# The rounded parts of q and k made on GpSimd instead of ScalarE in 22 attention steps

## The chip, the core and the metric

The kernel runs on one core of a Trainium2 chip. A core has five engines, each with its own instruction queue, that meet only at semaphores: TensorE (PE in the profile, with its weight loads as PEld), VectorE (DVE), ScalarE (ACT), GpSimd (POOL) and SyncE (SP), which here only issues DMAs. The metric is the time of one execution on the device, in microseconds. The kernel before took 996.66 us, the median of three runs (995.94 to 996.84).

## The reference

Attention with a sigmoid in the place of the softmax, and behind it a feed-forward layer with a squared ReLU:

```python
# q, k, v: (8, 12, 448, 64)
scores = scale * np.matmul(q, k.transpose(0, 1, 3, 2)) - np.log(S)
attn = 1.0 / (1.0 + np.exp(-scores))
attn_out = np.matmul(attn, v)
# x: 3584 tokens of 768; w_in (768, 2048), w_out (2048, 768)
h = x @ w_in
r = np.maximum(h, 0.0)
g = s * (r * r) + b
return g @ w_out
```

All of it is in float32 precision. The change touches only the attention.

## The kernel before

TensorE multiplies matrices in a rounded 32-bit format here (`F32R`, fp32r in the profile). To keep float32's precision, an operand x is split in two parts: hi, which is x rounded to that format, and lo = x - hi. A product is then made of three matmuls, hi by hi, hi by lo and lo by hi (`PARTS`, line 39).

The work has three stages. First comes attention, in 24 steps; during it the weights of the feed-forward layer, which come in 64-bit floats, are converted, combined and stored as parts, by ACT and DVE, in jobs that a hand-written plan gives to the steps (`at_step`, `ticks`, lines 534 to 540). Then the feed-forward layer is computed for one block of 512 tokens (lines 825 to 875), while the conversion ends. Last, it is computed for twice three blocks of 512 tokens (lines 992 to 1303), in a scheme that needs fewer products at the price of sums. The last two stages use neither q nor k.

A step of attention handles one batch and four of its heads. Its q and k lie in one tile of 128 x 2 x 2 x 448 numbers (`load`, line 387): two heads in the two halves of the partitions, two pairs of heads, q and k. The tile is fetched by one DMA on SP's queue two steps ahead (line 669) into a pool of two buffers. From it, one step ahead, the two parts are made:

- `parts_hi` (lines 409 to 413) allocates the tiles hi and lo, 128 x 1664 each (q, and the first three chunks of 128 keys; the rest of the keys is multiplied unsplit), and writes hi. The pool `hl` has one buffer for each (line 379), so hi of the next step can be written only when the scores of this step are done.
- `parts_lo` (lines 415 to 417) writes lo on DVE (the subtraction is `sub`, line 198).

The first two steps have their parts made on DVE (`parts_dve`, line 419). The other 22 (`TWO`, line 61) use the two functions above.

In step n (lines 650 to 687) instructions are issued in this order, and each engine takes its own in that order:

1. DVE's planned jobs of the step (line 652).
2. `scores` (line 439): TensorE makes 36 score matmuls from hi and lo in pairs (line 459), and ACT the sigmoids of the six chunks (lines 434 and 436).
3. `parts_hi` for step n + 1 (line 666), on ACT behind the six sigmoids.
4. ACT's planned jobs (line 667): converting weights (line 223), rounding weights and sums (lines 273 and 331).
5. DMAs on SP: q and k of step n + 2 (line 669), weights, and stores of finished weights.
6. TensorE's attention times v (line 495), the last scores of step n + 1 (line 481, whose sigmoid ACT does next), and the rest of attention times v (line 504).
7. `parts_lo` for step n + 1 (line 683), on DVE.
8. `store_x` (line 509): DVE takes two results from PSUM (line 512), SP stores them.

So on DVE lo stands behind the planned jobs and ahead of the two copies of line 512. GpSimd has no instruction in this loop. Synchronisation is derived from the tiles: whoever reads hi waits for whoever wrote it.

Of the kernel before, what the change touches and what calls it, by code (L numbers as in the profile page):

```python
# [102 lines left out]
def sigmoid_attention_relu2_ffn(  # L103
# [10 lines left out]
    nc = tc.nc  # L114
# [291 lines left out]
    def flat(x):  # L406
        return x.rearrange("p i x s -> p i (x s)")[:, :, :NX]

    def parts_hi(b, t, ld_):

        hi, lo = (hl.tile([P, 2, NX], F32R, tag=h, name=f"qk{h}_{b}_{t}") for h in "hl")
        nc.scalar.copy(hi, flat(ld_[0]))  # L412
        ld_.append((hi, lo))

    def parts_lo(ld_):
# [234 lines left out]
    for n, (b, t) in enumerate(quads):  # L650
# [4 lines left out]
        if n == 0:  # L655
            parts_dve(*quads[1], loaded[1], [(i, slice(NX)) for i in range(2)])
            ticks(0, "DVE")
            firsts = []

            def between():  # L660
                firsts.append(scores_last(*quads[0], loaded[0]))
                ticks(0, "ACT")

        else:
            if n + 1 in TWO:
                parts_hi(*quads[n + 1], loaded[n + 1])
            ticks(n, "ACT")
# [674 lines left out]
```

## Time and profile before

| what | value |
|---|---|
| median of three runs | 996.66 us (995.94 to 996.84) |
| span of the profiled execution | 995.0 us |
| attention: first 24 steps | to about 245 us |
| length of a step | 9.99 us |
| granted TensorE clock | 1.000 |
| copies of line 412 | 22, 35.6 us in all, 1617 ns in the mean |
| subtractions for lo in those steps | 22, 1892 ns in the median |
| DMA of a tile of q and k | 896 KB, 7.2 us to landing in the median |

The profile is of one execution. Its own time is known by its span, from the first to the last instruction; the median of the timed runs is 1.66 us above it. PE, PEld, DVE, ACT, POOL and SP are the engines. "L412" is line 412 of the kernel. A row of groups reads: line, engine, operation, output<-inputs, shapes, number of instructions | busy us in all, mean ns of one | idle us of the engine just before them, and who ended most of that idle time. A row of the timeline reads: start, duration, engine, line, operation, output<-inputs, shapes, count, and in brackets the idle time before it and its releaser. A row of waits reads: who waited <- for whom: us in total, times, longest. A row of the chain of waits reads: start, duration, engine, tile and line. A row of windows reads: the stretch and its length, then each engine's busy us (and number of instructions), the granted clock, the DMA engines' busy share and GB/s.

In the tile names qk is the raw tile of q and k, qkh is hi, qkl is lo, psc are scores, a are attention weights, pav is attention times v and xo its copy in SBUF; st and wf are weights in conversion, and t and w are sums and parts of weights.

### The profile page before, as it was taken

The page shows a single profiled execution, that of the slowest core. Times are in us where ns is not written, and L with a number is a line of the kernel's source. Part 1 is how long each engine was busy: PE and PEld are TensorE (multiplying, and loading weights), DVE is VectorE, ACT ScalarE, POOL GpSimd, SP SyncE. Part 2 cuts the span into 40 slices and gives each one's busy share as a digit, 9 for nine tenths or more (in the row PEclk, how much of TensorE's full clock was granted, in tenths as well). Part 3 has the DMA queues.
Part 4 walks back from the last instruction along what each step waited for, and adds up shares of the span by engine and source line. Part 5 has one row for each costly group of instructions (what it writes and reads, how often), then busy time and mean ns, then how long its engine had stood idle before and what let it go on. Part 6 is the DMA issues. An engine that isn't in the chain of part 4 may idle for free.

```text
span 995.0 us, 13973 instructions
## 1 busy us (share of the span) xinstructions
PE 991.2 (100%) x5288; PEld 783.6 (79%) x5288; DVE 840.6 (84%) x933; ACT 616.1 (62%) x687; POOL 0.2 (0%) x4
## 2 busy tenths in 40 slices
PE   9999999999999999999999999999999999999998
PEld 4555555555888888888888888888888888888887
DVE  5999999999889976799999898996465789889787
ACT  7999999998877575575455444443455336543432
POOL 0000000000000000000000000000000000000000
PEclk9999999999999999999999999999999999999999
DMA  8788898999899999999686678978666676677773
GB/s 327 282 332 324 311 372 316 418 359 402 306 404 360 371 391 407 381 334 368 215 276 204 210 260 309 305 249 267 202 207 198 205 208 197 209 239 226 229 240 123
DMA packets 101826, 287.18 MB, mean 289 GB/s; under 512 B 10240, under 2 KB 20608, under 8 KB 101760
## 3 DMA queue, kind: packets, MB, share of 16 engines
q1 hardware_dynamic: 101472, 285.84, 81.9%
q8 instruction: 42, 0.69, 0.3%
q10 hardware_dynamic: 288, 0.46, 0.1%
q14 instruction: 24, 0.20, 0.0%
HBM read 198.18 MB, written 88.08 MB: 288 GB/s over the span
## 4 chain that ended last, share of the span: by engine, by line
PE 100%; DVE 0%; issue 0%
PE o L1269 31%; PE h L1137 31%; PE pav L495 11%; PE psc L459 9%; PE po L811 6%; PE ph L606 6%; PE psc_l L481 2%; PE pav L504 2%; PE psc L465 0%; PE idle L527 0%; DVE C_t L198 0%
## 5 line engine op out<-in xcount | busy, mean ns | idle before, releaser
L1137 PE MATMUL h<-s_1h,wu 128*128 128x512 f32 x480 | 143.0, 379 | 0.0
L1137 PE MATMUL h<-s_0h,wu 128*128 128x512 f32 x480 | 143.0, 379 | 0.0
L436 ACT ACTIVATE a<-psc,nls 128x896 f32<-128x896 f32 x120 | 113.4, 1020 | 11.0 <-PE psc L459 8.3
L495 PE MATMUL pav<-a,v 128*64 128x448 f32 x576 | 113.8, 543 | 0.0
L1137 PEld LDWEIGHTS h<-s_0h,wu 128*128 128x128 f32 x480 | 90.7, 189 | 12.8
L1137 PEld LDWEIGHTS h<-s_1h,wu 128*128 128x128 f32 x480 | 90.7, 189 | 12.8
L1009 ACT COPY G<-h 128x1024 f32<-128x1024 f32 x48 | 48.9, 1019 | 82.3 <-PE h L1137 56.6
L901 ACT ACTIVATE G<-G,b_sb,s_sb 128x1024 f32<-128x1024 f32 x48 | 59.7, 1244 | 57.6 <-DVE G L898 57.0
L1137 PE MATMUL h<-s_0l,wu 128*128 128x512 f32 x240 | 91.0, 379 | 0.0
L1137 PE MATMUL h<-s_1l,wu 128*128 128x512 f32 x240 | 91.0, 379 | 0.0
L495 PEld LDWEIGHTS pav<-a,v 128*64 128x64 f32 x576 | 39.1, 137 | 62.6 <-issue 55.7
L195 DVE TENSOR_TENSOR G<-G,h 128x1024 f32<-128x1024 f32 x40 | 48.8, 1219 | 35.9 <-PE h L1137 34.7
L1269 PE MATMUL o<-g_3h,wu 128*128 128x512 f32 (+1 forms) x244 | 76.4, 376 | 0.0
L1269 PE MATMUL o<-g_0h,wu 128*128 128x512 f32 x240 | 76.3, 379 | 0.0
L1269 PE MATMUL o<-g_1h,wu 128*128 128x512 f32 x240 | 76.3, 379 | 0.0
L1269 PE MATMUL o<-g_2h,wu 128*128 128x512 f32 x240 | 76.3, 379 | 0.0
L811 PE MATMUL po<-g,w 128*128 128x512 f32 x288 | 64.8, 379 | 0.0
L811 PEld LDWEIGHTS po<-g,w 128*128 128x128 f32 x288 | 54.4, 189 | 8.0 <-DVE g L198 0.4
L606 PE MATMUL ph<-x0h,w 128*128 128x512 f32 x192 | 59.6, 380 | 0.0
L459 PE MATMUL psc<-qkh 64*128 64x448 f32 x282 | 53.8, 378 | 0.0
L198 DVE TENSOR_TENSOR qkl<-qk,qkh 128x1664 fp32r<-128x1664 f32 (+3 forms) x26 | 44.9, 1726 | 9.8 <-ACT qkh L412 9.5
L1269 PEld LDWEIGHTS o<-g_3h,wu 128*128 128x128 f32 x244 | 45.9, 189 | 6.4
(154 smaller groups left out, 2053.7 us busy)
## 6 DMA issues: line engine op xcount, KB each, us to landing
wu<-wd SPq DMA_DIRECT2D x240, 512.0 KB, 4.3
wd<-t SPq DMA_DIRECT2D x36, 768.0 KB, 8.0
qk<-qk_t SPq DMA_DIRECT2D x23, 896.0 KB, 7.2
st<-w_out SPq DMA_DIRECT2D x16, 768.0 KB, 8.6
st<-w_in SPq DMA_DIRECT2D x16, 768.0 KB, 8.6
wd<-w SPq DMA_DIRECT2D x16, 768.0 KB, 5.6
v<-v_t SPq DMA_DIRECT2D x24, 448.0 KB, 5.8
xd<-xo SPq DMA_DIRECT2D x24, 448.0 KB, 5.2
```

The costliest lines, as they stand in the source:

```text
L195: nc.vector.tensor_tensor(o, x, y, op=ALU.add)
L198: nc.vector.tensor_tensor(o, x, y, op=ALU.subtract)
L436: nc.scalar.activation(a, psc[:, :, :S], AF.Sigmoid, bias=nls, scale=SCALE)
L459: nc.tensor.matmul(o[j][:, :S], two[wi][r, i, cols], paired(two[xi][r, i, :S]), start=m == 0, stop=m == 2,)
L481: nc.tensor.matmul(psc[half[i], j, :S].rearrange("p (b a) -> p a b", a=2), x[r, i, 1, 3 * P :], x[r, i, 0, :], start=True, stop=True,)
L495: nc.tensor.matmul(pav[i][r, :S], ld_[1][:, 3 * i + c, j, :], a[i, c][:, j, :], start=c == 0, stop=False,)
L606: nc.tensor.matmul(ph, w[:, k, wi, kc * P : (kc + 1) * P], paired(x0[h][xi][:, cc, :]), start=m == 0, stop=m == 3 * NCC - 1,)
L811: nc.tensor.matmul(pos[e], w[:, k, wi, kc * P : (kc + 1) * P], paired(g[:, gi, :]), start=first and i == 0, stop=last and i == 2,)
L901: nc.scalar.activation(x, x, AF.Identity, bias=b_sb, scale=s_sb)
L1009: nc.scalar.copy(g(m, h), bk)
L1137: nc.tensor.matmul(bk[:, j], wt[:, j, wi, c * P : (c + 1) * P], paired(opd[i][xi][:, c, :]), start=i == ch[0] and m == 0, stop=m == 3 * KC ...
L1269: nc.tensor.matmul(o, wt[:, f, wi, e * P : (e + 1) * P], paired(g[gi][:, f, tk]), start=(end or i == ch[0] and p == 0) and f == 0 and m == ...
```

## The change

One line differs. The rounded copy hi of the next step's q and k is issued on GpSimd; what it reads, what it writes and where it stands in the program are the same.

```diff
     def parts_hi(b, t, ld_):
 
         hi, lo = (hl.tile([P, 2, NX], F32R, tag=h, name=f"qk{h}_{b}_{t}") for h in "hl")
-        nc.scalar.copy(hi, flat(ld_[0]))
+        nc.gpsimd.tensor_copy(hi, flat(ld_[0]))
         ld_.append((hi, lo))
```

`parts_hi` is called from one place, line 666, in steps 1 to 22, for the steps after them. So ACT's queue goes from the sixth sigmoid straight to its planned jobs, GpSimd gets 22 instructions, and `parts_lo` on DVE waits for GpSimd where it waited for ACT.

## Prediction

> **What bounds the kernel now.** I read the page first: span, busy time, and the slices.
>
> ```profile
> span 995.0 us, 13973 instructions
> PE 991.2 (100%) x5288; PEld 783.6 (79%) x5288; DVE 840.6 (84%) x933; ACT 616.1 (62%) x687; POOL 0.2 (0%) x4
> ...
> DVE  5999999999889976799999898996465789889787
> ACT  7999999998877575575455444443455336543432
> POOL 0000000000000000000000000000000000000000
> ```
>
> TensorE is busy throughout. ACT's 62% is a mean over unlike stages: in the first ten slices, the attention, ACT and DVE are both near full. POOL runs four instructions in all. So I read the stage, in windows of one attention step each; the first and last of 21, and their sum:
>
> ```profile
> core 0: us, PE busy (x) PEld busy (x) DVE busy (x) ACT busy (x) POOL busy (x), PEclk, DMA share, GB/s
> 26.40:36.39 9.99, 9.99 (x80) 5.38 (x76) 9.71 (x13) 9.35 (x12) 0.00 (x0) 1.00 0.80 298
> ...
> 226.16:236.15 9.99, 9.99 (x80) 5.39 (x76) 8.77 (x11) 9.45 (x12) 0.00 (x0) 1.00 1.03 405
> sum 209.75, PE 209.75 PEld 113.21 DVE 196.29 ACT 200.78 POOL 0.00; mean PE 9.99 PEld 5.39 DVE 9.35 ACT 9.56 POOL 0.00
> ```
>
> A step lasts 9.99 us, TensorE fills it at full clock, ACT has 0.43 us over (9.99 - 9.56) and DVE 0.64 (9.99 - 9.35). Three engines are within 7% of each other, so an engine that is given work, or is held up, can become the bound at once. The timeline of one step shows what hangs on what:
>
> ```profile
> 126.33 0.46 PE L459 MATMUL psc<-qkh 64*128 64x448 f32 x2
> 126.44 1.16 DVE L512 COPY xo<-pav 128x448 f32<-128x448 f32 x2
> 127.51 0.95 DVE L225 SCALAR_TENSOR_TENSOR wf<-st,wf 128x768 int32<-128x768 int32 x1
> 128.49 0.59 DVE L228 TENSOR_SCALAR st<-st 128x768 int32<-128x768 int32 x1
> 128.52 0.51 SPq L396 DMA_DIRECT2D qk<-qk_t  x1
> 129.11 0.96 DVE L232 SCALAR_TENSOR_TENSOR st<-st 128x768 f32<-128x768 uint32 x1
> 129.76 0.35 PE L459 MATMUL psc<-qkh,qkl 64*128 64x448 f32 x2
> 130.11 0.96 DVE L235 SCALAR_TENSOR_TENSOR wf<-st,wf 128x768 f32<-128x768 f32 x1
> 130.99 0.95 DVE L198 TENSOR_TENSOR t<-t 128x768 fp32r<-128x768 f32 x1
> 132.82 1.61 ACT L412 CAST qkh<-qk 128x1664 fp32r<-128x1664 f32 x1
> 133.44 0.55 DVE L219 TENSOR_SCALAR wf<-st 128x768 int32<-128x768 int32 x1
> 134.47 1.89 DVE L198 TENSOR_TENSOR qkl<-qk,qkh 128x1664 fp32r<-128x1664 f32 x1 [0.47 <-ACT qkh L412]
> 136.37 0.46 PE L459 MATMUL psc<-qkh 64*128 64x448 f32 x2
> 136.66 0.35 PE L459 MATMUL psc<-qkl,qkh 64*128 64x448 f32 x2
> ```
>
> ACT's copy ends at 132.82 + 1.61 = 134.43, DVE's subtraction for the second part (qkl) starts 0.04 later, ends at 136.36, and TensorE begins the next step's scores at 136.37; its second pair needs qkl. The chain copy, subtraction, scores is all but on the path, though TensorE itself still sets the pace.
>
> How late may qkl be? The steps whose subtraction started late tell: 9.98 to 9.99 us after the last is the rule, and one came 10.18 us after it (114.44 to 124.62, about 0.19 late). The attention-times-v matmuls after it came 10.03 us after those before, where 9.99 is the rule:
>
> ```profile
> 114.44 1.89 DVE L198 TENSOR_TENSOR qkl<-qk,qkh 128x1664 fp32r<-128x1664 f32 x1 [0.49 <-ACT qkh L412]
> 124.62 1.89 DVE L198 TENSOR_TENSOR qkl<-qk,qkh 128x1664 fp32r<-128x1664 f32 x1 [0.33 <-ACT qkh L412]
> ```
> ```profile
> 110.09 4.66 PE pav L495 x24
> 120.08 4.66 PE pav L495 x24
> 130.11 4.66 PE pav L495 x24
> 140.10 4.66 PE pav L495 x24
> ```
>
> So 0.19 us late cost TensorE 0.04: the slack is about 0.15 us a step.
>
> **The change part by part.** What goes from ACT, and what DVE idles for it:
>
> ```profile
> L412 ACT CAST qkh<-qk 128x1664 fp32r<-128x1664 f32 x22 | 35.6, 1617 | 0.0
> L198 DVE TENSOR_TENSOR qkl<-qk,qkh 128x1664 fp32r<-128x1664 f32 (+3 forms) x26 | 44.9, 1726 | 9.8 <-ACT qkh L412 9.5
> L624 DVE CAST x0h<-x0l 128x1536 fp32r<-128x1536 f32 x1 | 1.0, 951 | 0.0
> ```
>
> ```profile
> ACT a L436 <- PE psc L459: 8.3, 21, 0.6
> ```
>
> Removed: 22 copies of 1.617 us, 35.6 us of ACT. Worth nothing by itself: ACT waits for TensorE's scores at the start of a step already (8.3 us in 21 steps, by the waits), and TensorE has no gap in the windows above that an earlier sigmoid could fill. At most the 0.04 us of the one late step returns.
>
> Added: 22 copies on GpSimd, whose queue holds nothing else in the stage, so its waits block nothing behind them. When can one start? Its input was requested a step ahead (128.52 for use in the step from 136.37) and takes 7.2 us in the median, so it is there at 135.7. Its output buffer is single, and is free when the last score pair has read it: 129.76 + 0.35 = 130.11 in the step shown.
>
> ```profile
> qk<-qk_t SPq DMA_DIRECT2D x23, 896.0 KB, 7.2
> ```
>
> DVE is through with the work ahead of the subtraction at 133.44 + 0.55 = 133.99. So the copy may take 3.9 us at no cost, and up to 134.47 + 0.15 - 130.11 = 4.5 us before TensorE waits, if it runs beside DVE without touching it.
>
> What one copy lasts on GpSimd, no row shows: its four instructions are memsets of one element. From the nearest rows: below, DVE's one-input cast scaled, 0.951 x 1664 / 1536 = 1.03 us; above, twice ACT's row, 3.23 us, a factor I choose because these rows for such elementwise work already lie nearly a factor of two apart. I take 1.89 us, the slowest instruction of this shape in the trace (the subtraction), since the copy reads and writes the same array at one number at a time as that one does. All these fit in 4.5 us.
>
> [...]
>
> So duration alone costs nothing. What decides is whether the copy takes time from DVE. Between 130.11 and 133.99 DVE works without a break, and every instruction there reads its operands from the same memory as the copy. The rows say how much DVE takes in: the 768-element subtraction at 130.99 reads two operands in 0.95 us, and the one-input cast of 1536 elements also takes 0.95. In both, some 1536 numbers in 0.95 us: DVE draws on two streams in either form, so it has no spare one to give up for free. If the two engines take turns, it does not matter who goes first: DVE either stands while the copy runs, or the copy waits until DVE has nothing to do but wait for it (133.99) and then runs alone. Either way a copy's length is added to DVE's step.
>
> [...]
>
> The sum: DVE must find 22 x 1.89 = 41.6 us. It has free what it idles for qkh today, 9.5 us (the other 0.2 us of a step are gaps between dependent instructions, which stay). The slack of qkl, 22 x 0.15 = 3.3 us, goes against two hand-overs a step (0.04 us was the one from ACT above; two engines taking turns can hardly have cheaper ones, so 2 to 4 us); I set both to nothing. Added: 41.6 - 9.5 = 32.1 us. The profiled execution spans 995.0; the median of the timed runs, 996.66, lies 1.66 above it, which I keep: 995.0 + 1.66 + 32.1 = 1028.7 us. A step becomes about 9.99 + 32.1 / 22 = 11.45 us. Behind the late subtraction on DVE stand the two evictions (L512) and the weight conversion; who waits are TensorE's next scores. The stages after attention are not touched.
>
> With the ends of the copy's price: 1.03 gives 22.7 - 9.5 = 13.2, so 1009.9; 3.23 gives 71.1 - 9.5 = 61.6, so 1058.2.
>
> **The rivals.** First, not slower: the copy runs beside DVE undisturbed. It then lasts from 130.11 to about 132.0, the subtraction starts at about 134.0 instead of 134.47, and nothing follows, for TensorE is still busy with attention times v until 136.3: 996.6 us. For it: no row shows the two engines in conflict, and 1.89 is far under 4.5. Against: it must be nearly complete. A loss to DVE of 0.67 us a step (22 x 0.67 = 14.7, less 9.5 free and 3.3 slack, leaves 2) already shows, a third of one copy. From that point it decides.
>
> Second: undisturbed, but the copy lasts over 4.5 us. At 5.5 it would be 22 x 1.0 more, 1018.7 us; it needs a price 2.9 times the chosen one. The step would be set by GpSimd, with DVE idle.
>
> Third: faster. Lightening ACT by 35.6 us would have to bring TensorE forward, which has nothing to regain in the windows; I see under 1 us. That the copy does not go to GpSimd I leave out: the line names the engine.
>
> **How the numbers follow.** Turns between DVE and GpSimd 0.80, because a third of full exclusion is enough and DVE works without a break where the copy must run; undisturbed and in time 0.14; undisturbed and too slow 0.04; faster 0.02. A measurement of this kernel can tell 0.2%, 2 us, from no change. So faster 0.02, same 0.14, slower 0.84. The forecast is 1028.7 us. Its own range is 1010 to 1058, by the copy's price, and leaves out the undisturbed case and the tails, more than 2 in 10; so the whole range reaches down to that case: 996 to 1058.
>
> **What would show it.** Right: POOL with 22 casts that lie beside no two-input DVE instruction, or DVE instructions between 3.8 us and 7.7 us of a step that are longer or start late; the subtraction waiting for POOL's copy or starting over 1 us late; weight loads of the scores waiting for the subtraction; steps of 11 to 12 us; ACT idle by 3 us a step; the time after attention unchanged. Wrong: steps still of 9.99 us with POOL's copies beside DVE's rows of unchanged length (first rival), or DVE rows unchanged and idle for over 1 us before the subtraction while a POOL row fills more than 4.5 us (second).

## The result, and the profile after

The changed kernel takes 1010.86 us (median of 4 runs, 1010.21 to 1011.47), beside 996.75 us for the kernel before on the same chip: a ratio of 1.0141, 95% interval 1.0127 to 1.0156. It is slower, as forecast and, as the experiments below show, for the reason forecast, but by 14.1 us where 32 were forecast.

The page of the changed kernel, busy times and slices:

```profile
span 1008.7 us, 13955 instructions
PE 996.6 (99%) x5288; PEld 783.5 (78%) x5288; DVE 866.1 (86%) x933; ACT 585.3 (58%) x665; POOL 44.8 (4%) x26
...
DVE  5999999999889986699999899896555789989787
ACT  6786877777777766565536453443445436543432
POOL 1121121121000000000000000000000000000000
```

ACT has lost 31 us of work, POOL has got 45, and DVE, to which the change gave nothing, is busy 25.5 us longer (866.1 against 840.6). Two steps of the timeline show where:

```profile
126.33 1.57 POOL L412 CAST qkh<-qk 128x1664 fp32r<-128x1664 f32 x1 [8.28 <-PE psc L459]
126.50 1.83 DVE L228 TENSOR_SCALAR st<-st 128x768 int32<-128x768 int32 x1
...
131.13 0.55 DVE L219 TENSOR_SCALAR wf<-st 128x768 int32<-128x768 int32 x1
131.59 1.89 DVE L198 TENSOR_TENSOR qkl<-qk,qkh 128x1664 fp32r<-128x1664 f32 x1
...
133.53 0.46 PE L459 MATMUL psc<-qkl,qkh 64*128 64x448 f32 x2 [0.56 <-DVE qkl L198]
...
137.05 0.96 DVE L235 SCALAR_TENSOR_TENSOR wf<-st,wf 128x768 f32<-128x768 f32 x1
...
137.15 2.29 POOL L412 CAST qkh<-qk 128x1664 fp32r<-128x1664 f32 x1 [9.24 <-PE psc L459]
137.92 2.33 DVE L198 TENSOR_TENSOR t<-t 128x768 fp32r<-128x768 f32 x1
140.17 0.41 DVE L195 TENSOR_TENSOR t<-wf 128x256 f32<-128x256 f32 x1
```

In the first step POOL's copy starts at 126.33 and lasts 1.57 us, and the L228 that starts just after it takes 1.83 us. The same instruction in the kernel before:

```profile
120.39 0.56 DVE L228 TENSOR_SCALAR st<-st 128x768 int32<-128x768 int32 x1
```

In the second step the copy finds L235 running until 138.01, its record lasts 2.29 us, 1.43 us of it after that, and the next instruction on DVE, the subtraction of line 198, takes 2.33 us instead of 0.95 (the row at 130.99 of the kernel before). So it goes in all 22 steps: exactly one DVE instruction is longer, fifteen times one with two inputs, by 1.37 us, and seven times L228, with one input, by 1.23 to 1.26. Together 15 x 1.37 + 7 x 1.25 = 29.3 us. All other DVE instructions of the attention keep their length within 0.06 us.

Nothing waits for the copy any more: the subtraction at 131.59 has no idle time ahead of it, and starts before the row ahead of it has ended. TensorE does wait, for the subtraction (0.56 us at 133.53; the waits say "PEld psc L459 <- DVE qkl L198: 13.6, 20, 1.2"). The stretch from the end of the first of the 22 subtractions to that of the last, in windows, first of the kernel before:

```profile
core 0: us, PE busy (x) PEld busy (x) DVE busy (x) ACT busy (x) POOL busy (x), PEclk, DMA share, GB/s
26.46:236.22 209.76, 209.76 (x1600) 113.21 (x1596) 196.30 (x252) 200.79 (x230) 0.00 (x0) 1.00 0.90 344
```

and of the kernel after:

```profile
26.19:250.02 223.83, 215.53 (x1602) 113.14 (x1598) 220.53 (x253) 171.44 (x209) 42.24 (x21) 1.00 0.86 323
```

DVE was idle for 13.5 us (209.76 - 196.30) and is now for 3.3: DVE sets the pace of the steps, and the stretch is 14.1 us longer. That is the whole of the change's cost; from the end of that stretch to the end of the span it is 758.8 us before (995.0 - 236.22) and 758.7 after (1008.7 - 250.02).

### The profile page after: what moved, and what is told of

It is laid out like the page before. It is cut to its first block, busy times and chain, and to the rows that moved or that the text cites. A ratio compares the mean times of both kernels' runs of the same rounds, so it can differ in the third digit from the quotient of the medians.

```text
span 1008.7 us, 13955 instructions
## 1 busy us (share of the span) xinstructions
PE 996.6 (99%) x5288; PEld 783.5 (78%) x5288; DVE 866.1 (86%) x933; ACT 585.3 (58%) x665; POOL 44.8 (4%) x26
## 4 chain that ended last, share of the span: by engine, by line
PE 79%; DVE 18%; issue 2%; DMA 1%; DVEq 0%; SPq 0%
PE o L1269 31%; PE h L1137 31%; PE po L811 6%; PE ph L606 6%; DVE qkl L198 4%; DVE wf L225 3%; DVE t L198 2%; DVE st L232 2%; DVE xo L512 2%; PE pav L495 2%; DVE st L228 2%; PE psc L459 2%; DVE wf L235 1%; DVE wf L219 1%; DMA v<-v_t 1%
## 5 line engine op out<-in xcount | busy, mean ns | idle before, releaser
L495 PE MATMUL pav<-a,v 128*64 128x448 f32 x576 | 113.8, 543 | 0.0
L495 PEld LDWEIGHTS pav<-a,v 128*64 128x64 f32 x576 | 39.1, 137 | 62.7 <-issue 55.7
L223 ACT ACTIVATE wf<-wf,e_bias 128x768 int32<-128x768 int32 x32 | 29.2, 933 | 55.3 <-DVE wf L219 55.3
L459 PE MATMUL psc<-qkl,qkh 64*128 64x448 f32 x282 | 51.8, 364 | 8.2 <-DVE qkl L198 8.1
L459 PE MATMUL psc<-qkh 64*128 64x448 f32 x282 | 53.9, 379 | 0.1
```

What stands on the lines that cost most here:

```text
L459: nc.tensor.matmul(o[j][:, :S], two[wi][r, i, cols], paired(two[xi][r, i, :S]), start=m == 0, stop=m == 2,)
L495: nc.tensor.matmul(pav[i][r, :S], ld_[1][:, 3 * i + c, j, :], a[i, c][:, j, :], start=c == 0, stop=False,)
```

## Experiments

The first four ask whether it is the copy itself that costs, what ScalarE's lighter load is worth, and which of their instructions hold each other up. The kernel before took 996.58 us beside them (19 runs).

**A copy that nobody reads.**

```diff
         nc.scalar.copy(hi, flat(ld_[0]))
+        nc.gpsimd.tensor_copy(lo, flat(ld_[0]))
```

> ScalarE makes the rounded part as in the kernel before; GpSimd makes a second copy of the same input at the same time, into the tile of the low part, which the subtraction overwrites; nobody reads it. Theory (GpSimd's copy and VectorE's instructions take turns, VectorE is the bound): one VectorE instruction a step is 1.25 to 1.37 us longer, as in the changed kernel, time 1009 to 1012 us. Rival A (the rounded part arrives late, through GpSimd's start and its semaphores): the copy has no reader, so 996.7 us. Rival B (the copy's traffic slows the memory for all): as the theory in time, but many instructions, on ScalarE too, a little longer.

Measured: 1011.15 us (ratio 1.0144, 1.0129 to 1.0159), as much as the change itself. Its timeline (all lines behind 412 are one higher):

```profile
137.40 0.96 DVE L235 SCALAR_TENSOR_TENSOR wf<-st,wf 128x768 f32<-128x768 f32 x1
137.51 2.28 POOL L413 CAST qkl<-qk 128x1664 fp32r<-128x1664 f32 x1 [9.26 <-PE psc L460]
138.27 2.32 DVE L198 TENSOR_TENSOR t<-t 128x768 fp32r<-128x768 f32 x1
140.14 1.62 ACT L412 CAST qkh<-qk 128x1664 fp32r<-128x1664 f32 x1
142.10 0.55 DVE L219 TENSOR_SCALAR wf<-st 128x768 int32<-128x768 int32 x1
142.57 1.88 DVE L198 TENSOR_TENSOR qkl<-qk,qkh 128x1664 fp32r<-128x1664 f32 x1
```

The same instruction is stretched by the same 1.37 us, and ACT's copy lies there at its old length. Rival A, a late rounded part, is out. The edit alone doesn't exclude it, for the subtraction overwrites what GpSimd wrote and so must wait for GpSimd's copy here too; the rows do: the subtraction at 142.57 starts before the row ahead of it has ended, as in 21 of the 22 steps here and in all 22 of the changed kernel. DVE never waits for the copy. Rival B, traffic that slows all, is out too: one DVE instruction a step is longer, the rest are not (within 0.07 us), and none of ScalarE's is longer by more than 0.05.

**Nothing in ScalarE's place.**

```diff
-        nc.scalar.copy(hi, flat(ld_[0]))
+        if b == 0 and t == 2:
+            nc.scalar.copy(hi, flat(ld_[0]))
```

(the tile hi is then allocated once and kept).

> The rounded part is made once, by ScalarE in step 1, and used in all later steps, so that 21 of the 22 copies are left out and nothing stands in their place (the products of those steps are then wrong). Theory: ScalarE's 35 us are worth nothing, since TensorE sets the pace: 996.7 us, within 1 us. Rival (ScalarE's chain sigmoid, copy, subtraction sets the pace): 990 us or less.

Measured: 996.81 us, ratio 1.0001 (0.9991 to 1.001). Taking this work from ACT, for free, gains nothing.

**GpSimd writes but doesn't read.**

```diff
         nc.scalar.copy(hi, flat(ld_[0]))
+        nc.gpsimd.memset(f32(lo), 0.0)
```

> As the kernel before, and GpSimd fills the tile of the low part with zeros at the place where the changed kernel copies; it writes as many bytes and reads none. Theory in its narrow form (what the two engines share is the way by which they read): no two-input VectorE instruction is longer, one with one input (L228) may be; 996.7 to 998 us. Theory in its wide form (they exclude each other whatever GpSimd does): one instruction a step is longer by the length of the fill, about 1.4 us, 1009 to 1012 us. Rival B (traffic): half the bytes, about half the loss, 1003 us.

Measured: 1001.57 us (ratio 1.0049, 1.0032 to 1.0066): neither of the theory's two forms in time, and yet in its rows what the narrow one expected. Two places of the timeline:

```profile
122.61 1.48 POOL L413 MEMSET qkl<- 128x1664 f32 x1 [8.50 <-PE psc L460]
122.84 1.67 DVE L228 TENSOR_SCALAR st<-st 128x768 int32<-128x768 int32 x1
...
143.33 0.96 DVE L235 SCALAR_TENSOR_TENSOR wf<-st,wf 128x768 f32<-128x768 f32 x1
143.35 1.49 POOL L413 MEMSET qkl<- 128x1664 f32 x1 [8.50 <-DVE st L232]
144.21 1.82 DVE L198 TENSOR_TENSOR t<-t 128x768 fp32r<-128x768 f32 x2
```

The fill at 143.35 runs right across L235 and the subtraction, both with two inputs, and neither is longer (two subtractions in 1.82 us here). The fill at 122.61 holds up L228 by 1.1 us (1.67 instead of 0.56). That happens in seven steps, by 1.07 to 1.11 us, and in no other place, so rival B, traffic, is not in the rows here either. So the copy, which reads, held up two-input instructions by 1.37 us, and the fill, which only writes, by nothing; the one-input L228, which takes about 0.57 us where two-input instructions of the same size take 0.96, was held up by the fill too.

My number was off because I took the free time as a sum. It can be used only in the step in which it lies: six steps became longer, by 0.45 to 0.96 us, 4.6 in all, and the free time of the others was of no help. This comes back below.

**The same copy at another time.**

```diff
             if n + 1 in TWO:
+                old = flat(loaded[n][0])
+                nc.gpsimd.tensor_copy(old.bitcast(F32R), old)
                 parts_hi(*quads[n + 1], loaded[n + 1])
```

> As the kernel before, and GpSimd makes a copy of the same size each step, at another time: in place on the raw tile of the present step, right after its subtraction, while VectorE takes its two results from PSUM for some 1.1 us. Theory (turns only with instructions that read SBUF through the shared way): the PSUM copies keep their 0.62 us, only the instruction after them is longer, by 0.4 to 0.6 us, which fits in the 0.65 us that VectorE has free a step: 996.7 to 998 us. Rival B (traffic) and the wide form (any VectorE instruction): 1009 to 1012 us.

Measured: 998.25 us (ratio 1.0016, 1.0007 to 1.0026).

```profile
147.59 1.16 DVE L512 COPY xo<-pav 128x448 f32<-128x448 f32 x2
147.79 1.58 POOL L667 CAST qk<-qk 128x1664 fp32r<-128x1664 f32 x1 [8.43 <-PE pav L504]
148.66 1.52 DVE L225 SCALAR_TENSOR_TENSOR wf<-st,wf 128x768 int32<-128x768 int32 x1
```

The two PSUM copies keep their 1.16 us with GpSimd's copy beside them; only the instruction after them is longer, by 0.57 us here, by 0.33 to 0.69 over the steps. A GpSimd copy of the same size costs 1.7 us at this place (998.25 - 996.58) and 14.6 at the other (1011.15 - 996.58). The 1.7 us lie a little above what I expected: six steps became longer, by 0.09 to 0.40 us, 1.3 in all, and here too the free time of the others did not help.

The next four turn the dose up and down and move other work. The kernel before took 996.42 us beside them (10 runs).

**Half the copy.**

```diff
-        nc.scalar.copy(hi, flat(ld_[0]))
+        nc.gpsimd.tensor_copy(hi[:, 0], flat(ld_[0])[:, 0])
+        nc.scalar.copy(hi[:, 1], flat(ld_[0])[:, 1])
```

> GpSimd makes the rounded copy of the first pair of heads (half the tile), ScalarE that of the second. Theory: VectorE loses a little over half as much, 0.65 to 0.75 us a step, against some 0.65 us that it has free: 996.7 to 999.5 us. A loss in proportion to the work on GpSimd, with nothing free, would give half of 14 us, 1003.8 us.

Measured: 999.19 us (ratio 1.003, 1.0019 to 1.0041), a fifth of the full cost for half the copy.

```profile
131.22 0.96 DVE L235 SCALAR_TENSOR_TENSOR wf<-st,wf 128x768 f32<-128x768 f32 x1
131.32 1.60 POOL L412 CAST qkh<-qk 128x832 fp32r<-128x832 f32 x1 [9.25 <-PE psc L460]
132.09 1.63 DVE L198 TENSOR_TENSOR t<-t 128x768 fp32r<-128x768 f32 x1
```

The subtraction is 0.68 us longer. Half the elements cost half of 1.37, so by these two sizes the loss goes by elements, (1.37 - 0.68) / 832 = 0.83 ns each, with no fixed part.

**Two copies.**

```diff
         nc.gpsimd.tensor_copy(hi, flat(ld_[0]))
+        nc.gpsimd.tensor_copy(lo, flat(ld_[0]))
```

> The changed kernel with a second copy of the same input behind the first, into the tile of the low part. Theory: what VectorE loses doubles, 2.6 to 2.75 us a step, nothing is free any more: 996.7 + 22 x (2.65 - 0.65) = 1040.7 us, 1037 to 1043. If the turns are had by whole instructions, two VectorE instructions a step are longer by 1.2 to 1.4 us, or one by 2.8. Rival B (traffic): about the same in sum, but spread over many instructions.

Measured: 1038.79 us (ratio 1.0422, 1.0405 to 1.044).

```profile
139.26 1.58 POOL L412 CAST qkh<-qk 128x1664 fp32r<-128x1664 f32 x1 [7.29 <-PE psc L460]
139.44 1.83 DVE L228 TENSOR_SCALAR st<-st 128x768 int32<-128x768 int32 x1
140.79 1.92 POOL L413 CAST qkl<-qk 128x1664 fp32r<-128x1664 f32 x1
141.31 2.21 DVE L232 SCALAR_TENSOR_TENSOR st<-st 128x768 f32<-128x768 uint32 x1
```

Copy, DVE instruction, copy, DVE instruction: turns by whole instructions. The second copy costs 27.9 us (1038.79 - 1010.86), 1.27 a step, for with the first all free time is gone.

**The copy on VectorE.**

```diff
-        nc.gpsimd.tensor_copy(hi, flat(ld_[0]))
...
         hi, lo = ld_[-1]
+        nc.vector.tensor_copy(hi, flat(ld_[0]))
         sub(lo, flat(ld_[0]), f32(hi))
```

> VectorE makes the rounded copy itself, right ahead of the subtraction; neither ScalarE nor GpSimd does. Theory (VectorE is the bound once it loses more than it has free, and the time follows from what it loses): a copy of 1.03 us (0.951 us for 1536 elements, scaled) instead of a loss of 1.30 us: 22 x (1.03 - 0.65) = 8.4 us, 1004 to 1006 us, less than on GpSimd. Rival A (the path through GpSimd is what costs): 996.7 us.

Measured: 1004.76 us (ratio 1.0084, 1.0069 to 1.0099).

```profile
138.72 1.02 DVE L416 CAST qkh<-qk 128x1664 fp32r<-128x1664 f32 x1
139.78 1.89 DVE L198 TENSOR_TENSOR qkl<-qk,qkh 128x1664 fp32r<-128x1664 f32 x1
```

DVE makes the copy in 1.02 us, less than the 1.33 it loses in the mean to GpSimd's (29.3 / 22). As a way to relieve ScalarE, GpSimd is worse here than DVE itself, and neither pays.

**A PSUM copy moved to ScalarE**, on top of the change:

```diff
-            nc.vector.tensor_copy(
+            (nc.scalar.copy if i else nc.vector.tensor_copy)(
                 o[:, i].rearrange("p (a b) -> p a b", a=2),
```

> The changed kernel, with one of the two PSUM copies of each step (0.62 us) moved from VectorE to ScalarE, which has 1.6 us more free than before. Theory (VectorE is the bound, GpSimd's copy costs it 1.30 us a step): 22 x (1.30 - 0.58 - 0.65) = 1.5 us over the kernel before, 997 to 1000 us. Rival A (the rounded part is late): the subtraction does not start earlier, 1010 to 1012 us.

Measured: 1002.95 us (ratio 1.0065, 1.005 to 1.008). The time falls by 8, so rival A is out once more, but it stays 3 to 6 us over what I expected. I put that on ScalarE's later sigmoids, and left the PSUM copy out altogether, to see:

```diff
-        for i in range(2):
+        for i in range(1):
...
-        nc.sync.dma_start(x_dram[b][:, 2 * t : 2 * t + 2], o)
+        nc.sync.dma_start(x_dram[b][:, 2 * t : 2 * t + 2], o[:, :1].to_broadcast([P, 2, S]))
```

> The changed kernel, with the second of the two PSUM copies of each step left out and nothing in its place (the store sends the first result twice, so half of the attention's output is wrong); ScalarE is not given any of it. Theory: VectorE loses 1.33 us a step, of which 0.55 to 0.6 comes back and 0.69 is free: 22 x (1.33 - 0.57 - 0.69) = 1.5 us, 997 to 999 us; what the version with the copy on ScalarE lay above that, some 4 us, came from ScalarE's later sigmoids, which free the score buffers 0.25 us later. If those 4 us are a loss of VectorE that the theory has not counted: 1001 to 1004 us.

Measured: 1001.30 us (ratio 1.0047, 1.003 to 1.0063; before 996.46). My explanation fell: what the copy on ScalarE costs over none at all is some 1.65 us (1002.95 - 1001.30), not 4, and with two ratios known to 0.0015 each it is not clear of noise. The rest is the same mistake as with the fill. The lengths of seven steps (2 to 8), each from the start of a step's first L495 matmul to that of the next:

```
kernel before     9.98   9.99   9.99   9.99   9.99   9.99   9.99
changed          11.03  10.53  10.26  10.80  10.58  11.21  10.79
one PSUM copy    10.51  10.29   9.99  10.32  10.06  10.68  10.27
```

A PSUM copy left out takes 0.53 us from DVE's step (1.15 for two less 0.62 for one), and steps fall by about that, but never below TensorE's 9.99. Taking 0.53 from each of the changed kernel's steps, with 9.99 as the floor, leaves 3.7 us over the kernel before; the steps of the version without the copy add up to 4.1 over it, and the medians differ by 4.8 (1001.30 - 996.46). The rest of about 1 us I leave open. The mean step of my expectation gave 1.5.

## Why the prediction was right in direction and wrong in size

**What bounds the kernel.** Right. ScalarE's 35 us are worth nothing (0.9991 to 1.001), and with the copy on GpSimd the bound passes to DVE.

**When the copy can start.** Right in what releases it: in 21 of the 22 steps the copy starts some 0.1 us behind the last score pair that reads the buffer, in one it waited for the DMA of q and k instead. That is at 3.8 us of a step only in the first two, as forecast; in the others it is 4.1 to 5.0 us, for the scores ahead of it now wait for the subtraction.

**Turns.** Right, and this was the one thing the trace of before could not show. That DVE has nothing to give up for free was my inference from two of its rows (some 1536 numbers in 0.95 us, with one input and with two). The runs show who is held up: two-input DVE instructions by GpSimd's copy (1.37 us) and not by its fill (L235 kept 0.96), L228 by both (1.25 and 1.09 us in the mean), and copies from PSUM not by the copy (1.16 us for two); no fill ran beside those. Why L228 differs from the two-input instructions, and what the two engines share, no run shows.

**The price of a copy.** This step failed. "I take 1.89 us, the slowest instruction of this shape in the trace": the copy alone lasts 1.57, and DVE loses 1.33 in the mean (29.3 / 22), since 0.2 us of the copy's record do not hold it up. The bounds I had set, 1.03 and 3.23, hold it; the choice within them was bad. That the subtraction, with two inputs on another engine, tells the length of a one-input copy on GpSimd was a guess, and the runs did not bear it out. The price too high makes 22 x (1.89 - 1.33) = 12.3 us of the miss. ScalarE's row for the very same copy, 1.62, was the nearer one.

**What DVE has free.** This step failed as well: 9.5 us, "the other 0.2 us of a step are gaps between dependent instructions, which stay", and the slack of qkl and the hand-overs "both to nothing". Of the 29.3 us lost, 15.2 were swallowed (29.3 - 14.1). Over the 21 steps of the windows above, 27.9 us are lost (29.3 less the first step's 1.37) and the stretch grows by 14.1. Idle time covers 10.2: the wait for qkh, and some 2 us of waits before the PSUM copies. Of the other 3.7 (27.9 - 14.1 - 10.2), some 2.9 are no idle time at all: a DVE row that follows another without a wait starts about 0.08 us before that one's end (131.59 against 131.13 + 0.55 = 131.68), and where an idle gap closes, that much is gained. The last 0.8 are many other rows that are shorter by up to 0.06 us each. Hand-overs, which I had set against the slack, cost nothing beyond the 1.33. The free time too low makes 15.2 - 9.5 = 5.7 us of the miss.

With both terms as measured the sum is 996.7 + 29.3 - 15.2 = 1010.8, where 1010.86 was measured. This is no forecast, for the 15.2 was found from the measured growth. Both terms had been wrong towards a slower kernel, so their errors added up. And that the measured time lies within the range, near 1009.9, the sum for a copy of 1.03 us, is no support for that price: DVE lost 1.33 us a step and swallowed more of it than the 9.5 us.

**The rivals.** The undisturbed copy and the copy that is too slow are both out: in no step does DVE wait for the copy, and its rows are not of unchanged length. The third, faster, is out with the measured time: ScalarE's lighter load returns nothing.

## What to carry to other kernels

Before work goes to an idle engine, ask whose instructions it will hold up: here GpSimd's copy was paid for by VectorE (1.33 us a step), the engine with 6% to spare, and VectorE would have made the copy itself for less (1.02 us). Look at the very instructions that will lie beside it: a GpSimd copy that began beside copies from PSUM cost 1.7 us, one of the same size that lay wholly beside SBUF arithmetic 14. And count free time step by step, with the other engine's time as a floor; what one step has over is of no use to the next.

## What the runs showed of the hardware that was not expected

- GpSimd got its turn although DVE's instructions follow one another without a wait: its copy waited for the instruction that ran (0.86 us at 137.15), and the next DVE instruction waited for the copy (2.33 us instead of 0.95). Neither engine was held up for more than one instruction of the other at a time, even with two copies in a row (the second, at 140.79, began 0.48 us before the end of L228).
- The record of GpSimd's copy includes that wait: 1.57 us at 126.33, where L225 had 0.13 us left to run, 2.29 at 137.15, where L235 had 0.86. The mean of its group, 2026 ns, is neither the copy's length nor what it costs.
- A fill of the same size took 1.48 us on GpSimd, and two-input instructions of DVE beside it kept their length (0.96 us for L235 at 143.33).
- DVE's copies from PSUM and GpSimd's copy in SBUF ran side by side with both at their usual length (0.62 and 1.57 us).
